# Threshold search moved beside the expert layers: experts run in the order in which they fill, weights by run-time index, token lists by products, the 64-row block in two column groups

## The chip, the cores and the metric

The kernel runs on one core of one Trainium2 chip. Times are device microseconds (us) of one execution. PE is TensorE, PEld its weight load, DVE is VectorE, ACT is ScalarE, POOL is GpSimd.

## The reference

An attention block makes 4608 token vectors of 512 numbers. They are then dealt out to eight experts, each with room for exactly 576 tokens, in the order of all 36,864 scores. Each expert is two matrix products with a ReLU between them. Everything is float32.

```python
def _attn_ref(q, k, v, g_norm):            # q, k, v: (8, 8, 576, 64)
    kv = np.einsum('bhsd,bhse->bhde', k, v)
    out = np.einsum('bhsd,bhde->bhse', q, kv)
    rms = np.sqrt(np.mean(out * out, axis=-1, keepdims=True) + 1e-06)
    return (out / rms * g_norm).astype(np.float32)

def _moe_ref(x, w_gate, w1, w2):           # x: (4608, 512), 8 experts, w1 512x1024, w2 1024x512
    cap = N // E                           # 576
    logits = x @ w_gate
    order = np.argsort(-logits.flatten())
    for idx in order:
        tok, e = (int(idx) // E, int(idx) % E)
        if assigned[tok] >= 0 or counts[e] >= cap:
            continue
        assigned[tok] = e
        counts[e] += 1
    for e in range(E):
        mask = assigned == e
        h = np.maximum(x[mask] @ w1[e], 0.0)
        out[mask] = h @ w2[e]
```

## The kernel before

The kernel never sorts. It does the dealing in eight rounds. In a round each token looks at its best expert that still has room (`choose`). A search then finds the score at which the first expert becomes full (`threshold`), and every choice above that score is accepted (`assign`). So one more expert is full at the end of each of the first seven rounds, and the eighth takes what is left. The search narrows an interval [lo, hi] in eight steps of 16 candidates: DVE compares every token with every candidate, PE counts by 36 small bf16 products (one for each column of 128 tokens), and DVE picks the new interval.

```python
NCAND = 16
NSTEP = 8
# [...] attention; the weights of experts 0 and 1 are requested during it
def threshold():
    lo, hi = bottom, top
    for _ in range(NSTEP):
        step = small("step")
        nc.vector.tensor_scalar(step, in0=hi, scalar1=lo, scalar2=(1.0 + 2.0 ** -18) / (NCAND + 1),
                                op0=AL.subtract, op1=AL.mult)
        cand = small("cand", NCAND)
        nc.vector.tensor_scalar(cand, in0=cand_n, scalar1=step, scalar2=lo, op0=AL.mult, op1=AL.add)
        over = asg.tile([P, GC, NCAND], BF, name="over", tag="over", bufs=2)
        nc.vector.tensor_tensor(over, ..., op=AL.is_ge)      # 36 x NCAND comparisons a partition
        n_ps = psr.tile([NCAND, E], FT, name="n_ps", tag="n", bufs=2)
        for c in range(GC):
            nc.tensor.matmul(n_ps, lhsT=over[:, c, :], rhs=best[:, :, c], start=(c == 0), stop=(c == GC - 1))
        # [...] full, n_full, some: which candidates leave an expert full
        nc.tensor.matmul(k_ps, lhsT=ones_b[0:NCAND, :], rhs=some, start=True, stop=True)
        nc.vector.tensor_scalar(up, in0=k_ps, scalar1=1.0, scalar2=step, op0=AL.add, op1=AL.mult)
        nc.vector.tensor_scalar(hi2, in0=up, scalar1=lo, scalar2=hi, op0=AL.add, op1=AL.min)
        nc.vector.tensor_scalar(lo2, in0=k_ps, scalar1=step, scalar2=lo, op0=AL.mult, op1=AL.add)
        lo, hi = lo2, hi2
    return lo, hi

for _ in range(E - 1):
    choose()
    assign(*threshold())
choose()
# [...] the rest; then the lists of all experts at once by 36 place comparisons and products
gather(0)
gather(1)
turn(0)                                   # transposes of the gathered rows
for e in range(E):
    # first layer: 16 groups of four products, 128x128 by 288, into h_ps
    # turn(e + 1), gather(e + 2)
    for n, (a, nr) in enumerate(blocks):  # second layer: blocks of 128, 128, 128, 128, 64 rows
        for f in range(FC):               # FC = 8
            nc.tensor.matmul(y_ps[0:nr, :], lhsT=hid[:, f, a:a + nr], rhs=w2[:, f, :],
                             start=(f == 0), stop=(f == FC - 1))
        # [...] copy, scatter of the rows to the output
    if e + 2 < E:
        load_w(e + 2)
```

## Time and profile before

| | before |
|---|---|
| median of 4 runs, us | 1035.39 (1034.42 to 1037.18) |
| span of the profiled run, us | 1034.2 |
| attention, us | 0 to 174 |
| search and lists, first gather, us | 174 to 481 |
| experts, us | 481.0 to 1024.2, 67.9 each |
| PE busy over the span | 73% |

The profile has a page with one row per engine over 40 equal slices of the span, a view by stretches and a timeline. A timeline line reads: start, duration, engine, source line, operation, output and inputs, sizes, how many instructions were merged. In brackets stands how long the engine had been idle just before, and what ended the wait. Products are named by the tile that they write, `h_ps` in the first layer and `y_ps` in the second, for example. Merged durations run to the end of the last instruction, which overlaps the next group, so I take costs from start to start. A float32 product shows as two instructions.

### The profile page before, as it was taken

The numbers are of one execution on the slowest core, as the hardware profiler recorded it, in microseconds if no ns is written. First come the engines' busy times: TensorE is split into PE (matmuls) and PEld (weight loads), VectorE is DVE, ScalarE is ACT, GpSimd is POOL, SyncE is SP. The second block draws the span as 40 slices with busy tenths as digits, with TensorE's granted clock in tenths as the row PEclk, the third lists the DMA queues.
The fourth block names the chain that finished last, engine by engine and source line by source line (L and its number), as shares of the span: only waits on it lengthen the run. The fifth ranks groups of instructions, "written<-read, shape, count | busy, mean of one in ns | idle before, by whom it ended". The sixth has DMA issues, their size and how long they took to land.

```text
span 1034.2 us, 13718 instructions
## 1 busy us (share of the span) xinstructions
PE 750.4 (73%) x5917; PEld 499.6 (48%) x5917; DVE 341.8 (33%) x1060; ACT 104.1 (10%) x206; POOL 135.2 (13%) x117
## 2 busy tenths in 40 slices
PE   1888882322322322317999999999999999999996
PEld 1777772221221221215746647557466474574752
DVE  0277556567567567582101101101001011010100
ACT  0144432000000000000100101001011001010100
POOL 2144323000000000005020210211102101001001
PEclk9899996555555555556999999999999999999998
DMA  9998982000000000004032312321223112301000
GB/s 221 297 240 278 320 331 110 1 2 1 1 1 1 2 1 1 1 1 137 24 135 97 137 35 83 147 107 67 91 97 138 65 52 103 107 0 41 6 20 25
DMA packets 32572, 91.07 MB, mean 88 GB/s; under 512 B 2816, under 2 KB 2816, under 8 KB 32512
## 3 DMA queue, kind: packets, MB, share of 16 engines
q1 hardware_dynamic: 24832, 66.59, 19.5%
q0 software_dynamic: 6976, 23.60, 7.2%
q8 instruction: 46, 0.75, 0.3%
q10 hardware_dynamic: 704, 0.02, 0.1%
q14 instruction: 14, 0.11, 0.0%
HBM read 71.32 MB, written 18.87 MB: 87 GB/s over the span
## 4 chain that ended last, share of the span: by engine, by line
issue 49%; DVE 23%; PE 15%; POOL 7%; DMA 4%; ACT 1%; POOLq 0%; DVEq 0%; ACTq 0%
PE n_ps L310 6%; DVE over L305 4%; POOL out_dram L510 4%; DMA v_sb<-in_v_dram 3%; PE o_ps L162 3%; PE kv_ps L131 3%; POOL xg L469 2%; DVE cand L303 2%; DVE part L182 2%; DVE up L320 1%; DVE step L300 1%; DVE hi L322 1%; DVE lo L324 1%; PE qt_ps L155 1%; DVE full L313 1%
## 5 line engine op out<-in xcount | busy, mean ns | idle before, releaser
L506 PE MATMUL y_ps<-w_sb,hid 128*128 128x512 f32 (+1 forms) x640 | 280.2, 594 | 0.0
L496 PE MATMUL h_ps<-xt,w_sb 128*128 128x288 f32 x1024 | 252.3, 408 | 0.9 <-DVE hid L458 0.9
L496 PEld LDWEIGHTS h_ps<-xt,w_sb 128*128 128x128 f32 x1024 | 194.6, 191 | 60.1 <-issue 5.7
L506 PEld LDWEIGHTS y_ps<-w_sb,hid 128*128 128x128 f32 (+1 forms) x640 | 112.5, 179 | 151.3 <-issue 150.7
L310 PE MATMUL n_ps<-best,over 128*16 128x8 bf16 x2016 | 62.6, 176 | 146.3 <-DVE over L305 105.7
L310 PEld LDWEIGHTS <-over 128*16 128x16 bf16 x2016 | 56.9, 90 | 174.1 <-DVE over L305 172.4
L458 DVE TENSOR_SCALAR hid<-h_ps 128x288 f32<-128x288 f32 x64 | 29.2, 458 | 255.1 <-PE h_ps L496 255.1
L469 POOL DMA_INDIRECT xg<-x_dram,ids x40 | 38.1, 952 | 452.5 <-DVE ids L435 296.4
L510 POOL DMA_INDIRECT out_dram<-y_sb,ids x40 | 38.6, 966 | 323.1 <-ACT y_sb L456 189.3
L462 DVE COPY y_sb<-y_ps 128x512 f32<-128x512 f32 (+1 forms) x17 | 11.8, 691 | 208.3 <-PE y_ps L506 208.3
L131 PE MATMUL kv_ps<-v_sb,k_sb 64*64 64x64 f32 x1152 | 45.0, 240 | 27.5 <-DMA v_sb<-in_v_dram 25.9
L131 PEld LDWEIGHTS kv_ps<-v_sb,k_sb 64*64 64x64 f32 x1152 | 42.1, 154 | 30.8 <-issue 27.3
L162 PE MATMUL o_ps<-bd,qt 128*64 128x144 f32 x576 | 46.6, 304 | 10.9 <-DVE qt L157 8.9
L452 ACT ACTIVATE hid<-h_ps 128x288 f32<-128x288 f32 x64 | 26.3, 411 | 223.6 <-PE h_ps L496 223.6
L162 PEld LDWEIGHTS o_ps<-bd,qt 128*64 128x64 f32 x576 | 38.4, 144 | 15.0 <-ACT o_sb L166 8.8
L454 ACT ACTIVATE xt<-t_ps,g_col 128x512 f32<-128x512 f32 (+1 forms) x17 | 11.5, 675 | 324.0 <-PE t_ps L480 321.8
L305 DVE TENSOR_TENSOR over<-mx,cand 128x576 bf16<-128x576 f32 x56 | 42.3, 755 | 1.5
L456 ACT COPY y_sb<-y_ps 128x512 f32<-128x512 f32 (+1 forms) x23 | 13.4, 584 | 253.3 <-PE y_ps L506 253.3
L177 POOL TENSOR_TENSOR x_sb<-o_sb,inv 128x1536 f32<-128x1536 f32 x12 | 33.2, 2769 | 41.6 <-DVE inv L175 32.4
L313 DVE SCALAR_TENSOR_TENSOR full<-n_ps,goal 16x8 f32<-16x8 f32 x56 | 8.6, 153 | 67.7 <-PE n_ps L310 67.7
L480 PEld LDWEIGHTS t_ps<-ident,xg 128*128 128x128 f32 (+1 forms) x160 | 18.7, 149 | 17.9 <-issue 8.0
L460 DVE TENSOR_SCALAR xt<-t_ps,g_col 128x512 f32<-128x512 f32 (+1 forms) x23 | 15.4, 669 | 35.8 <-PE t_ps L480 33.8
(136 smaller groups left out, 471.2 us busy)
## 6 DMA issues: line engine op xcount, KB each, us to landing
w_sb<-in_moe_w_dram SPq DMA_DIRECT2D x16, 2048.0 KB, 9.7
k_sb<-in_k_dram SPq DMA_DIRECT2D x8, 1152.0 KB, 9.6
v_sb<-in_v_dram SPq DMA_DIRECT2D x8, 1152.0 KB, 17.8
x_dram<-x_sb SPq DMA_DIRECT2D x12, 768.0 KB, 4.3
q_sb<-in_q_dram POOLq DMA_DIRECT2D x4, 1152.0 KB
q_sb<-in_q_dram SPq DMA_DIRECT2D x4, 1152.0 KB, 17.3
xg<-x_dram,ids POOLq DMA_INDIRECT x40
out_dram<-y_sb,ids POOLq DMA_INDIRECT x40
```

The lines of the kernel that those rows point to most:

```text
L131: nc.tensor.matmul(kv_ps[ls, r, :], lhsT=k_sb[ls, r, j, :], rhs=v_sb[ls, r, j, :], start=(j == 0), stop=(j == R - 1))
L162: nc.tensor.matmul(o_ps[ps_, r, 0:W], lhsT=qt[:, r, ps_], rhs=bd[:, 2 * i + n, r], start=True, stop=True)
L177: nc.gpsimd.tensor_tensor(x_sb.rearrange("p (a l d) -> p a l d", l=2, d=D), o_sb.rearrange("p t r w -> p (t r) w")[:, :, 0:P].rearrange("p ...
L182: nc.vector.tensor_tensor(part, o_sb.rearrange("p t r w -> p (t r) w")[:, :, P:W].rearrange("p a (l e) -> p a l e", l=2), inv.rearrange("p ...
L305: nc.vector.tensor_tensor(over, mx.rearrange("p (c o) -> p c o", o=1).to_broadcast([P, GC, NCAND]), cand.rearrange("p (o n) -> p o n", o=1 ...
L310: nc.tensor.matmul(n_ps, lhsT=over[:, c, :], rhs=best[:, :, c], start=(c == 0), stop=(c == GC - 1))
L452: nc.scalar.activation(dst, src, ACT.Relu)
L458: nc.vector.tensor_scalar(dst, in0=src, scalar1=0.0, scalar2=None, op0=AL.max)
L469: nc.gpsimd.indirect_dma_start(out=xg[0:nr, :], out_offset=None, in_=x_dram, in_offset=bass.IndirectOffsetOnAxis(ap=ids[0:nr, e * NB + n:e ...
L496: nc.tensor.matmul(h_ps, lhsT=w1[:, d, f * P:(f + 1) * P], rhs=xt[:, d, cs], start=(d == 0), stop=(d == DC - 1))
L506: nc.tensor.matmul(y_ps[0:nr, :], lhsT=hid[:, f, a:a + nr], rhs=w2[:, f, :], start=(f == 0), stop=(f == FC - 1))
L510: put = nc.gpsimd.indirect_dma_start(out=out, out_offset=bass.IndirectOffsetOnAxis(ap=ids[0:nr, e * NB + n:e * NB + n + 1], axis=0), in_=y ...
```

## The change

The intent is to hide the search. An expert's tokens are known as soon as its round is over, so its layers can run while DVE looks for the next threshold. The order in which the experts run is then not known when the program is built, hence weights by an index that is read at run time. Five parts belong to it:

- The search takes 6 steps of 44 candidates in place of 8 of 16, and each step picks lo and hi from precomputed distances (`away`) by two selections, in place of five dependent small operations.
- Each expert gets its own token list, by a running count, a mask and five products (`fetch`).
- Control code is written as Python generators. The layers hand out an estimate of PE time after each product; when the estimated time of a `yield` is used up, the next piece of the search is put into PE's order. That order is then fixed.
- The transposes for the next expert (`turn`) stand together before the last block, and their eviction is on ACT alone.
- The last block of an expert has 64 rows; it is called the half block below. Its eight products are split into two sums of four, in two halves of the array's columns, and DVE adds the halves.

```diff
-NCAND = 16
-NSTEP = 8
+NCAND = 44
+NSTEP = 6
# [...] load_w and the weights' early loads in the attention go away
-        for _ in range(NSTEP):
-            step = small("step")
-            nc.vector.tensor_scalar(step, in0=hi, scalar1=lo, ...)
-            cand = small("cand", NCAND)
-            nc.vector.tensor_scalar(cand, in0=cand_n, scalar1=step, scalar2=lo, op0=AL.mult, op1=AL.add)
+        for s in range(NSTEP):
+            cand = small("cand", NCAND + 2)
+            nc.vector.tensor_scalar(cand[:, 0:NCAND + 1], in0=away[:, s], scalar1=lo, scalar2=None, op0=AL.add)
# [...]
+            nc.vector.tensor_copy(cand[:, NCAND + 1:NCAND + 2], hi)
+            yield 6.5 if s == 0 else 2.9
# [...] 36 products into n_ps; full, some
+            yield 0.9
# [...] k_ps; then up, hi2, lo2 go away for
+            nc.vector.scalar_tensor_tensor(at, in0=row_f[:, 0:NCAND + 1], scalar=k_ps, in1=cand[:, 0:NCAND + 1],
+                                           op0=AL.is_equal, op1=AL.mult, accum_out=lo)
# [...] and the same for hi
+    def fetch(t):
# [...] which expert has filled, its tokens, their running count kn
+        e = nc.sync.value_load(index[0:1, 0:1], min_val=0, max_val=E - 1)
+        w1 = wpool.tile([P, DC, F], FT, name="w1_sb", tag="w1")
+        for h in range(2):
+            fs = slice(h * F // 2, (h + 1) * F // 2)
+            nc.sync.dma_start(w1[:, :, fs], moe_w1[bass.ds(e, 1)]...)
+        w2 = wpool.tile([P, FC, DM], FT, name="w2_sb", tag="w2")
+        nc.sync.dma_start(w2, moe_w2[bass.ds(e, 1)].rearrange("o (a p) d -> p (o a) d", p=P))
+        yield 3.0
+        nc.tensor.matmul(a_ps, lhsT=before, rhs=kn[:, GC - 1:GC], start=True, stop=True)
# [...]
+        yield 2.4
+        for n in range(NB):
+            nc.tensor.matmul(s_ps[:, n], lhsT=of[:, n * P:(n + 1) * P], rhs=kn, start=True, stop=True)
# [...] ids from s_ps; five indirect gathers
+            if n == NB - 1 and t + 1 < E:
+                yield None                    # the turn of the next expert comes here
# [...] whole blocks as before; the block of 64 rows:
+                for f in range(FC // 2):
+                    for l in range(2):
+                        nc.tensor.matmul(y_ps[l * nr:(l + 1) * nr], lhsT=hid[:, l * FC // 2 + f, a:a + nr],
+                                         rhs=w2[:, l * FC // 2 + f, :], start=(f == 0), stop=(f == FC // 2 - 1))
+                nc.scalar.copy(y_part, y_ps[nr:2 * nr])
+                nc.vector.tensor_tensor(y_sb[0:nr], y_ps[0:nr], y_part, op=AL.add)
# [...]
+    for _ in control(0):
+        pass
+    for _ in turn(0):
+        pass
+    with tc.manual_schedule(engines={PE, DVE, Activation}):    # (names shortened)
+        for t in range(E):
+            ctl = control(t + 1) if t + 1 < E else None
+            wait = next(ctl, None) if ctl is not None else None
+            for used in layers(t):
+                if used is None:
+                    while wait is not None:
+                        wait = next(ctl, None)
+                    for _ in turn(t + 1):
+                        pass
+                    continue
+                if wait is not None:
+                    wait -= used
+                    if wait <= 0:
+                        wait = next(ctl, None)
```

## The prediction

> **What bounds the kernel now.** I read the page's slice rows first: they show three stages that barely overlap. In this fence each digit is one fortieth of the span (25.9 us).
>
> ```profile
> PE   1888882322322322317999999999999999999996
> DVE  0277556567567567582101101101001011010100
> PEclk9899996555555555556999999999999999999998
> DMA  9998982000000000004032312321223112301000
> ```
>
> Attention fills slices 0 to 6. Then come twelve slices in which PE is 20 to 30% busy at half the clock, DVE is 50 to 80% busy and DMA is at zero: the search for the eight experts' thresholds. Then PE is full to the end. The stretch view puts numbers on it (columns: stretch, length, busy time and count of PE, weight loads, DVE, ACT, POOL, then granted clock, DMA share, GB/s):
>
> ```profile
> 174.00:180.50 6.50, 0.66 (x2) 0.29 (x2) 6.07 (x35) 0.00 (x0) 0.16 (x1) 0.50 0.00 0
> 180.50:470.00 289.50, 79.78 (x2123) 67.18 (x2123) 195.71 (x756) 0.00 (x0) 0.00 (x0) 0.50 0.00 1
> 470.00:481.00 11.00, 6.01 (x23) 4.02 (x23) 1.50 (x2) 1.40 (x3) 7.97 (x9) 0.50 0.54 152
> 481.00:1024.20 543.20, 542.34 (x1802) 321.30 (x1802) 54.19 (x101) 49.84 (x102) 67.85 (x71) 1.00 0.22 78
> ```
>
> So 296 us go to setup, search and lists, 11 us to the first gather, 543 us to experts in which PE never waits (542.3 of 543.2), and 10 us to the last write. Search and experts stand in line only because the program orders them so: the first is a chain of small dependent steps, the second is bound by PE. One step of the search, from the timeline (start, duration, engine, line):
>
> ```profile
> 203.06 0.76 DVE L305 TENSOR_TENSOR over<-mx,cand 128x576 bf16<-128x576 f32 x1
> 203.87 1.12 PE L310 MATMUL n_ps<-best,over 128*16 128x8 bf16 x36 [2.05 <-DVE over L305]
> ...
> 205.03 0.15 DVE L313 SCALAR_TENSOR_TENSOR full<-n_ps,goal 16x8 f32<-16x8 f32 x1 [1.21 <-PE n_ps L310]
> ...
> 205.42 0.16 PE L318 MATMUL k_ps<-some,ones_b 16*128 16x1 bf16 x1 [0.43 <-DVE some L316]
> ```
>
> The comparison of the step before starts at 199.30, so a step takes 3.76 us. The last view is one expert on PE, again the timeline; matmuls of f32 are two instructions each:
>
> ```profile
> 549.50 0.14 PEld L506 LDWEIGHTS y_ps<-w_sb,hid 128*64 128x64 f32 x1 [0.29 <-issue]
> 550.45 31.31 PE L496 MATMUL h_ps<-xt,w_sb 128*128 128x288 f32 x128
> 585.55 33.03 PE L506 MATMUL y_ps<-w_sb,hid 128*128 128x512 f32 x76
> 618.50 1.72 PE L496 MATMUL h_ps<-xt,w_sb 128*128 128x288 f32 x6
> ```
>
> 550.45 to 618.50 is 68.05 us: 64 first-layer products at 0.487 (31.1), 40 second-layer products at 0.858 (34.3), 20 transposes in about 2.1, and gaps. The fifth block has 64 rows, yet its eight products start 0.43 us per instruction apart, just as full blocks do: 6.9 us for half the work.
>
> **What the Trainium skill says.** "TensorE: Matmul & The Clock Gate", Part 1, says that an idle PE is clocked at half and that about 3.4 us of sustained work releases it. The trace agrees: 0.50 in the search, 1.00 in the experts. Search products placed inside the expert stream should therefore run at full clock, while the first search stays at half. The same page, Part 2 (LDWEIGHTS), has the load cost grow with the columns of the stationary operand; the search's operand grows from 16 to 44 columns. At half clock the trace has 36 pairs in 1.12 us, 31 ns a pair, for 16 columns; no 44-column load is in it. Part 3 says that products of at most 64 output rows in different column groups run at once. The trace supports it: the attention's `o_ps` products (64 columns, 144 wide) alternate halves and 16 instructions take 1.20 us, 75 ns each, whereas 144 wide at the experts' 0.429 us per 512 would alone be 121 ns. "TensorEngine Tiling (Array Packing)", Key Properties, warns that a change of tiling mode drains PE; no row before isolates that, and I allow for it below.
>
> **The change part by part.**
>
> *First search, still exposed.* 44 candidates and six steps replace 16 and eight. The comparison grows from 576 to 1584 elements; the rows with 576 (755 ns) and 1440 elements (1651 ns) give 1.04 ns an element, so 1.80 us. The counting burst at half clock I put at 1.6 us (44-column load plus 8 columns, about 43 ns a pair). Counting and its follow-up (full, some, `k_ps`, two selections with accumulators, new candidates, a copy) are 1.6 us. A step is 5.05 us, six are 30.3. Setup grows from 6.5 to 8 us (a POOL iota and six `away` rows). The assignment takes 3.3 us to its product; then, because the scheduler weaves the next choose into it on DVE, 6.3 us to `a_ps`, 3.2 to `s_ps`, and 4.3 to the list, of which one 1.8 us comparison is woven in. That is 8 + 30 + 17 = 55 us from 174 us: list at 229. Gather and transposes then take 11 us as before: experts start at 240 instead of 481. Weights, which used to be fetched in the attention, are asked for some 10 us before the list is done; 4 MB land in about 20 us (9.7 us per 2 MB), about when they are needed. Lists for all experts at once (the 36 place comparisons and products, 457 to 470 us) go away.
>
> *Seven searches inside the experts.* They no longer add their chain, only their PE time and any wait at which PE's in-order stream meets an unfinished DVE step. PE time: six bursts at 1.25 us (36 pairs at some 30 ns, plus a drain at each end), six `k_ps` at 0.1, and the rest 0.5: 8.6 us. Waits: by the order of the built program, 14 first-layer products (6.8 us) stand before the first burst, against about 7.2 us of DVE (merge of the half block, choose, comparison); six products (2.9 us) against 2.9 between steps; five second-layer ones before `all_ps`, enough; four (3.4 us) before `a_ps`, against some 5.5 us of DVE. I take 3.0 us of waits.
>
> *Half block in two.* Sixteen instructions in pairs: about 3.8 us instead of 6.9.
>
> *Transposes together, evictions on ACT alone.* Five blocks through two banks at 0.69 us each on ACT, behind a 0.58 us output copy: 3.5 us instead of 2.1. ACT has about 13 us of work per expert, so it does not bound.
>
> Per expert: 31.0 + 27.5 (32 full products) + 3.8 + 3.5 + 8.6 + 3.0 = 77.4 us. Expert 0 pays about 2 us for the rising clock, as before; six with a search come to 466. Expert 6 carries only the remainder's list, whose `a_ps` stands after seven products (3.4 us) while DVE needs some 8.5: 72 us. Expert 7 carries nothing: 62.3. Together 600 us, against 543.
>
> *Tail.* 10.0 us before, plus 0.8 for the copy and addition of the two halves.
>
> Sum: 240 + 600 + 11 = 851 us; I say **850**. The search gives 241 us back, its presence among the experts costs about 82, the half block returns about 25 of that.
>
> **The rivals.** First, PE is the bound of the expert stage, so whatever is put there adds. If a burst drains PE at both ends or a 44-column load is not hidden, it costs 2 us instead of 1.25: 42 bursts add 32 us, 882. For: no such mix is in the trace, and mode changes drain. Against: the bursts run at full clock. Second, PE's order is now fixed; if DVE is late by 0.5 us at each of some 60 meeting points, that adds 30 us, and a gap beyond 3.4 us could halve the clock for a window. For: the budgets are close to my DVE sums. Against: each product of spacing only has to absorb what I counted. Third, weights by run-time index may land late, because they are asked for only some 48 us into the expert before (41 to `all_ps` and 7 of DVE and queue). 4 MB in 20 us end near 70, needed at 77: hidden, unless scatter and gather double it; then about 10 us per expert, 920. Fourth, the other way: the half block pairs well, bursts cost 1.0 us and waits vanish, and it is 820. A loss of the whole gain would need the experts to take 100 us each; nothing points to it.
>
> **Range and chances.** The first search is good to 8 us, the bursts to 15, waits to 12, the half block to 8; together about 25 either way, and the upper side has more ways. Range 825 to 885. Faster by over 2% means under 1014, which is 160 us away: 0.97. Within 2% 0.015, slower 0.015.
>
> **What would show it.** In the changed kernel's timeline: a step of the first search of 5 us and the first continuous `h_ps` near 240; granted clock 1.0 afterwards; expert to expert 77 us; a burst of 36 about 1.25 us between two `h_ps`; half block under 4 us; the waits on PE naming DVE mainly at `a_ps` and the first burst; no PE wait for `w_sb`. I am wrong if `h_ps` waits for weights, if a burst takes 2 us or more, if the half block still takes 6.9, or if the first search takes well over 55 us.

## The result, and the profile after

The changed kernel takes **847.8 us** (median of 4 runs, 847.21 to 848.48), the kernel before 1035.39. The ratio is 0.819 (95% interval 0.817 to 0.820). A ratio here is the mean time of one kernel's runs over the mean of the other's in the same rounds, so it is not quite the quotient of the medians.

The slice rows of the changed kernel's page (a slice is 21.2 us here):

```profile
PE   0689889513099999999999999999999997999995
DVE  0064854855725505633570555156235605000000
PEclk9899999855599999999999999999999998999998
DMA  9999892100610430070016005300800264200000
```

The stretch of sparse PE at half clock has shrunk from twelve slices to three. From the twelfth slice on PE is full at full clock, and DVE is busy beside it. The 7 in PE's row, near the end, is one slice in which something went wrong; it returns below. DMA is at 6 of 10 in the eleventh slice, where the kernel before had none: the first weights and the first rows.

The stretches (length, then busy time and count of PE, PEld, DVE, ACT, POOL, then clock, DMA share, GB/s):

```profile
174.00:184.22 10.22, 0.66 (x3) 0.29 (x3) 9.30 (x42) 0.00 (x0) 1.45 (x3) 0.50 0.00 0
184.22:210.28 26.06, 10.57 (x222) 9.73 (x223) 14.26 (x53) 0.00 (x0) 0.00 (x0) 0.50 0.00 1
210.28:231.00 20.72, 0.70 (x8) 0.39 (x8) 16.27 (x60) 0.00 (x0) 2.78 (x3) 0.50 0.54 197
231.00:237.30 6.30, 4.05 (x21) 3.34 (x21) 0.00 (x0) 2.55 (x4) 2.08 (x3) 0.59 0.60 207
237.30:835.70 598.40, 579.43 (x3191) 351.67 (x3190) 208.72 (x711) 96.01 (x204) 71.00 (x74) 0.99 0.22 79
```

The experts begin at 237.3 in place of 481.0: 243.7 us gained. They take 598.4 us in place of 543.2: 55.2 us given back. The tail is 10.3 in place of 10.0. That is the whole difference of the spans, 1034.2 to 846.0.

PE's timeline shows where the 55.2 us are. First two bursts of the exposed search, then a piece of the first expert with its bursts, then the end of that expert:

```profile
184.22 1.60 PE L323 MATMUL n_ps<-best,over 128*44 128x8 bf16 x36 [6.61 <-DVE over L316]
...
188.99 1.60 PE L323 MATMUL n_ps<-best,over 128*44 128x8 bf16 x36 [2.57 <-DVE over L316]
...
245.30 1.24 PE L506 MATMUL h_ps<-xt,w_sb 128*128 128x288 f32 x4
246.47 0.17 PE L332 MATMUL k_ps<-some,ones_b 44*128 44x1 bf16 x1
246.57 3.18 PE L506 MATMUL h_ps<-xt,w_sb 128*128 128x288 f32 x12
249.68 1.13 PE L323 MATMUL n_ps<-best,over 128*44 128x8 bf16 x36
250.74 1.24 PE L506 MATMUL h_ps<-xt,w_sb 128*128 128x288 f32 x4
...
284.05 0.16 PE L423 MATMUL a_ps<-know,before 128*128 128x1 bf16 x1 [1.70 <-DVE index L412]
...
307.55 1.04 PE L485 MATMUL t_ps<-ident,xg 128*128 128x128 f32 x8
...
310.80 3.65 PE L525 MATMUL y_ps<-w_sb,hid 128*64 128x512 f32 x16
```

An exposed step is 188.99 − 184.22 = 4.77 us. Among the layers the burst takes 250.74 − 249.68 = 1.06 us and the `k_ps` product 0.10. But the four `h_ps` instructions after a burst take 246.47 − 245.30 = 1.17 us, where four at the usual 0.243 would take 0.97, and the twelve after `k_ps` take 3.11, where twelve would take 2.92. So each excursion from the float32 stream to small products and back costs 0.2 us beside the products themselves, and a step costs PE 1.06 + 0.10 + 2 × 0.2 = 1.56 us.

Narrow windows of the same timeline show single instructions, and where the 0.2 us lie:

```profile
246.13 0.41 PE L506 MATMUL h_ps<-xt,w_sb 128*128 128x288 f32 x1
246.47 0.17 PE L332 MATMUL k_ps<-some,ones_b 44*128 44x1 bf16 x1
...
246.92 0.41 PE L506 MATMUL h_ps<-xt,w_sb 128*128 128x288 f32 x1
...
277.76 1.02 PE L517 MATMUL y_ps<-w_sb,hid 128*128 128x512 f32 x2
278.62 0.17 PE L363 MATMUL all_ps<-sums,ones_b 128*128 128x16 bf16 x1
```

About half is lost on the way in: `k_ps` starts 246.47 − 246.13 = 0.34 us after the last `h_ps`, where another `h_ps` starts after 0.243. The other half is lost on the way back: the first `h_ps` starts at 246.57, and the second 0.35 us later. The type is not what costs on the way in. `all_ps`, also bf16 but 128 by 128 like the stream, starts 0.43 us after the last `y_ps`, the usual distance; the `y_ps` after it costs 0.08. And the 28 `h_ps` that follow a float32 half block (314.39 to the next burst at 321.38) also take 0.2 us more than their 6.80, with no bf16 product before them. The loss on the way in thus goes with a change of the stationary operand's shape (44 columns, 44 rows or 64 columns in place of 128 by 128).

The turn takes 310.80 − 307.55 = 3.25 us. The half block takes 3.6 us; the next expert begins at 314.39. PE waits 1.70 us for DVE before `a_ps` in each of the first six experts, and no longer anywhere else in them than 0.4 us at the turn. The half blocks of experts 0 and 5 begin at 310.80 and 696.43, so one expert takes 385.63 / 5 = 77.13 us.

Expert 6, which prepares the last list without a search, has a gap:

```profile
700.02 3.66 PE L506 MATMUL h_ps<-xt,w_sb 128*128 128x288 f32 x14
708.32 0.16 PE L423 MATMUL a_ps<-know,before 128*128 128x1 bf16 x1 [4.64 <-DVE index L412]
708.34 5.15 PE L506 MATMUL h_ps<-xt,w_sb 128*128 128x288 f32 x10
713.28 0.37 PE L437 MATMUL s_ps<-know,of 128*128 128x39 bf16 x5
```

PE stands still for 4.64 us, and the next ten `h_ps` instructions take 5.15 us where ten take 2.67 without the gap (shown with an experiment below). The clock was halved: the view by stretches has 0.50 from 707.3 to 713.9 us, and 1.00 before and after. The gap costs about 7 us in all.

The sum of an ordinary expert, from these lines: 64 first-layer products 31.1, 32 whole second-layer products 27.5, half block 3.6, turn 3.25, six steps 9.4, other small products about 0.6, wait at `a_ps` 1.7. That is 77.1, against 67.9 before. Six such experts are 462.8, expert 6 takes 73.3, expert 7, beside which nothing runs, 62.3.

### The profile page after: what moved, and what is told of

Its sections match the earlier page's. It is cut to its first block, busy times and chain, and to the rows that moved or that the text cites. A ratio compares the mean times of both kernels' runs of the same rounds, so it can differ in the third digit from the quotient of the medians.

```text
span 846.0 us, 12815 instructions
## 1 busy us (share of the span) xinstructions
PE 714.9 (85%) x5410; PEld 470.7 (56%) x5410; DVE 332.4 (39%) x1033; ACT 152.1 (18%) x310; POOL 136.5 (16%) x119
## 4 chain that ended last, share of the span: by engine, by line
PE 59%; issue 16%; DVE 13%; DMA 6%; ACT 3%; POOL 2%; ACTq 0%; SPq 0%; POOLq 0%; DVEq 0%
PE h_ps L506 24%; PE y_ps L517 17%; PE n_ps L323 6%; DMA v_sb<-in_v_dram 4%; PE o_ps L162 3%; PE y_ps L525 3%; PE kv_ps L131 2%; DVE part L182 2%; DMA w_sb<-in_moe_w_dram 1%; DVE over L316 1%; DVE ms L167 1%; ACT xt L486 1%; PE qt_ps L155 1%; POOL out_dram L490 1%; PE t_ps L485 1%
## 5 line engine op out<-in xcount | busy, mean ns | idle before, releaser
L506 PE MATMUL h_ps<-xt,w_sb 128*128 128x288 f32 x1024 | 273.0, 417 | 0.0
L517 PE MATMUL y_ps<-w_sb,hid 128*128 128x512 f32 x512 | 224.6, 595 | 0.0
L517 PEld LDWEIGHTS y_ps<-w_sb,hid 128*128 128x128 f32 x512 | 95.8, 190 | 124.0 <-issue 123.2
L509 ACT ACTIVATE hid<-h_ps 128x288 f32<-128x288 f32 x128 | 52.5, 410 | 260.1 <-PE h_ps L506 258.5
L316 DVE TENSOR_TENSOR over<-mx,cand 128x1584 bf16<-128x1584 f32 x42 | 75.9, 1808 | 1.3
L323 PE MATMUL n_ps<-best,over 128*44 128x8 bf16 x1512 | 50.2, 178 | 19.5 <-DVE over L316 19.5
L323 PEld LDWEIGHTS <-over 128*44 128x44 bf16 x1512 | 46.1, 104 | 36.6 <-DVE over L316 22.7
L131 PE MATMUL kv_ps<-v_sb,k_sb 64*64 64x64 f32 x1152 | 43.0, 235 | 27.5 <-DMA v_sb<-in_v_dram 27.5
L520 ACT COPY y_sb<-y_ps 128x512 f32<-128x512 f32 x32 | 18.7, 585 | 216.3 <-PE y_ps L517 216.3
L485 PE MATMUL t_ps<-ident,xg 128*128 128x128 f32 (+1 forms) x160 | 23.2, 283 | 14.2 <-DMA xg<-x_dram,ids 9.8
L525 PE MATMUL y_ps<-w_sb,hid 128*64 128x512 f32 x128 | 29.2, 598 | 0.0
## 6 DMA issues: line engine op xcount, KB each, us to landing
w_sb<-in_moe_w_dram SPq DMA_DIRECT2D x8, 2048.0 KB, 17.3
```

The source lines that it names most:

```text
L131: nc.tensor.matmul(kv_ps[ls, r, :], lhsT=k_sb[ls, r, j, :], rhs=v_sb[ls, r, j, :], start=(j == 0), stop=(j == R - 1))
L316: nc.vector.tensor_tensor(over, mx.rearrange("p (c o) -> p c o", o=1).to_broadcast([P, GC, NCAND]), cand[:, 1:NCAND + 1].rearrange("p (o n ...
L485: nc.tensor.transpose(t_ps[:, d, 0:nr], xg[0:nr, d * P:(d + 1) * P], ident[0:nr, 0:nr])
L506: nc.tensor.matmul(h_ps, lhsT=w1[:, d, f * P:(f + 1) * P], rhs=xt[:, d, cs], start=(d == 0), stop=(d == DC - 1))
L509: nc.scalar.activation(hid[:, f, cs], h_ps, ACT.Relu)
L517: nc.tensor.matmul(y_ps, lhsT=hid[:, f, a:a + nr], rhs=w2[:, f, :], start=(f == 0), stop=(f == FC - 1))
```

## The experiments

Theory: the gain is the overlap alone. The search that is left beside the experts costs PE about 1.5 us a step, and the half block earns some of that back. Rivals: the gain comes from a cheaper search (44 candidates, six steps, new arithmetic), which would have helped the old order too; or it comes from the half block. Twelve kernels ran, on three chips, each set with runs of the kernel before on the same chip. The changed kernel itself ran only with its first set, so a difference from it below goes across chips; medians of the kernel before in the four sets lie within 1.1 us of each other (1034.3 to 1035.4). All twelve results agree with the reference, the one with the coarse search included.

### serial: the overlap alone undone

```diff
-            wait = next(ctl, None) if ctl is not None else None
+            if ctl is not None:
+                for _ in ctl:
+                    pass
+            wait = None
```

Everything else of the change stays, but each search runs to its end before the layers of the expert.

> The changed kernel with one thing undone: each search runs to its end before the layers of the expert before it start, so nothing of it lies beside the experts' products; every other part stays. Theory (the overlap is the gain): a search alone is about 48 us of chain (choose 4, six steps of 4.77, assignment and list some 15), against 11.7 us that it costs now among an expert's products (77.1 less 65.4 of pure work); six searches give +218, the remainder's list +8, and restarting at half clock +2 to 3 each, so about 1090 us. Rival (the gain comes from fewer steps, cheaper lists and the split half block, the overlap being eaten by contention on PE): 870 to 930 us.

Measured: 1050.93 us, ratio to before 1.015 (1.013 to 1.017). The timeline between expert 0 and expert 1 (the half block of the one, the first burst, the list, the layers of the next):

```profile
332.88 3.65 PE L525 MATMUL y_ps<-w_sb,hid 128*64 128x512 f32 x16
343.22 1.60 PE L323 MATMUL n_ps<-best,over 128*44 128x8 bf16 x36 [6.69 <-DVE cand L319]
...
378.24 0.16 PE L423 MATMUL a_ps<-know,before 128*128 128x1 bf16 x1 [5.47 <-DVE index L412]
```

The layers go on at 380.68, so the chain takes 44.2 us from the end of the half block at 336.5. I had expected 48. From it come off the 10 us of PE time and the 1.7 us of waits that an expert no longer has among its products, which leaves 32.5 us. The layers then start at half clock (0.50 from 380.7 to 385.2 us), as I had also counted on: the 128 first-layer products take 32.6 us in expert 0 and up to 34.1 later, where 31.1 is usual. So an expert with a search takes 111.1 to 112.5 us in place of 77.1, 34.0 to 35.4 more. Five of these (174.6) and a first expert that begins 32.3 us later are 207 us. The last list, for which I had expected 8 us more, gives 3.3 back, because expert 6 then has neither a gap nor a list among its products. The spans differ by 203.6. Of the 39 us that I had expected too much, about 26 lie in the six searches and 11 in the last list. What follows: the overlap is worth 203 us, more than the whole gain of 187. Without it, the rest of the change is slower than the kernel before.

### before_44x6 and before_newstep: the search alone, in the old order

The first puts 44 candidates and six steps into the kernel before, and nothing else. The second adds the new arithmetic (`away`, two selections).

```diff
-NCAND = 16
-NSTEP = 8
+NCAND = 44
+NSTEP = 6
```

> The kernel before with 44 candidates and six steps in place of 16 and eight, nothing else. Theory: a step grows from 3.76 to about 4.8 us, 42 in place of 56 steps, so 201 against 210 us of search: about 1026 us, 1% faster. Rival (fewer steps are what saved the time): 56 to 42 steps at an unchanged 3.76 would give 982 us.

Measured: 1048.1 us, ratio 1.012 (1.010 to 1.014). This is a miss in sign. The timeline of this kernel, two bursts:

```profile
188.10 1.60 PE L310 MATMUL n_ps<-best,over 128*44 128x8 bf16 x36 [3.11 <-DVE over L305]
...
193.42 1.60 PE L310 MATMUL n_ps<-best,over 128*44 128x8 bf16 x36 [3.12 <-DVE over L305]
```

A step is 5.31 us, not the 4.77 of the changed kernel: the old chain of small operations (`up`, `lo`, `hi`, `step`, `cand`) is still in it. 42 steps of 5.31 are 223 us, 56 of 3.76 were 211. A wider step costs more than the two steps it saves. The next kernel tests this reading.

> The kernel before with the whole step of the changed kernel: 44 candidates, six steps, and the two selections in place of five small dependent operations. Theory: a step is 4.77 us instead of the 5.31 of the run with 44 by six alone, so 42 steps are 200 us against 210 before, less a microsecond for setup: about 1026 us. Rival (the extra 13 us of that run came from elsewhere): about 1048.

Measured: 1028.14 us, ratio 0.995 (0.993 to 0.998), and a step of 4.77 us. So the new arithmetic takes 0.54 us out of a step, 23 us in 42 steps (20 us are measured against before_44x6, on another chip), and the two together bring the old order 6 us. The cheaper search explains next to nothing of the 187.

### sixteen_by_eight: the changed kernel with the old numbers

```diff
-NCAND = 44
-NSTEP = 6
+NCAND = 16
+NSTEP = 8
```

> The changed kernel with 16 candidates and eight steps, as before the change. Theory (a burst of 36 pairs costs PE nearly the same for 16 columns as for 44, so two more steps add 1.56 us each in six searches, 19 us; the first search is eight steps of about 3.2, 3 us shorter): about 864 us. Rival (the load's columns decide; a 16-column burst costs a good deal less than 1.06 us): 850 or below.

Measured: 866.92 us, ratio 0.838 (0.837 to 0.840), 19 us more than the changed kernel. Its burst among the layers:

```profile
327.81 1.12 PE L323 MATMUL n_ps<-best,over 128*16 128x8 bf16 x36
328.85 1.24 PE L506 MATMUL h_ps<-xt,w_sb 128*128 128x288 f32 x4
```

328.85 − 327.81 = 1.04 us for 16 columns, and 1.06 us for 44. At full clock the width of the candidates costs PE nothing, and the change to small products and back costs the same 0.2 us. An expert takes 80.8 us, 3.7 more: two steps at 1.56, and about 0.6 because the turn now waits for its rows. So 44 by 6 is worth its wider comparison only where the comparison is hidden. In the exposed first search of this kernel a step takes 3.16 us, so eight steps take 25.3 us where six of 4.77 take 28.6, and the first expert begins 4.1 us sooner, at 233.14. With the old arithmetic 44 by 6 lost in the old order too.

### three_steps: half the search

```diff
-    def threshold():
+    def threshold(steps):
# [...] and control(t) calls threshold(NSTEP if t == 0 else 3)
```

> The changed kernel with only three steps in the seven later searches (the first but all six of the first search remain); thresholds are too coarse, so the result is wrong on purpose, the lists stay valid. 18 steps go (six later searches of six steps hold steps: 36 to 18). Theory (each step adds its PE time to a stream that PE bounds, 1.56 us by the timeline: 1.06 burst, 0.11 second product, 0.2 at each of two re-entries into f32): 28 us less, about 820 us. With my predicted 1.35 us a step: 24 us less, 824. Rival (the bursts fill gaps of PE or DVE sets the pace): under 8 us less.

Measured: 817.98 us, ratio 0.790 (0.788 to 0.791), 29.8 us less. Divided by the 18 steps that went, this is 1.66 us each, but not all of it is theirs. From expert to expert it is 72.47 us in place of 77.13, which is 1.55 us a step: the 1.56 to which the timeline's terms add up, and not the 1.35 that I had predicted. The rest lies in the start (0.4 us) and in expert 6 (1.1 us), which has the same gap of 4.64 us but spends 3.4 us at half clock after it, where the changed kernel spends 6.8. On these inputs the result stayed within tolerance, but a threshold this coarse lets the order of tokens decide inside the last interval, so this is no usable version.

### half_whole: the split of the 64-row block undone

```diff
-            if nr == P:
+            if True:
-                    nc.tensor.matmul(y_ps, lhsT=hid[:, f, a:a + nr], rhs=w2[:, f, :],
+                    nc.tensor.matmul(y_ps[0:nr], lhsT=hid[:, f, a:a + nr], rhs=w2[:, f, :],
-                nc.scalar.copy(y_sb, y_ps)
+                nc.scalar.copy(y_sb[0:nr], y_ps[0:nr])
```

> The changed kernel with the 64-row block as eight whole products, as before. Theory: the split saves 6.9 less 3.6 us for each of eight experts, less 0.6 us of tail, so about 873 us. Rival (the second copy and the addition, or a drain at the mode change, give it back): within 5 us of 848.

Measured: 867.71 us, ratio 0.838 (0.837 to 0.840), 19.9 us more. The block in the timeline:

```profile
310.24 7.08 PE L517 MATMUL y_ps<-w_sb,hid 128*64 128x512 f32 x16
```

7.0 us in place of 3.6, 3.4 an expert, as expected, and 8 × 3.4 would be 27. The rest has another cause: here expert 6 has no gap at `a_ps` and takes 69.3 us, 4 less than in the changed kernel although its half block is longer. The split puts an addition of the halves into DVE's fixed order just ahead of the next list, so DVE can't begin that list before the half block is done; without the split it can. The split is a gain of 20 us net, and a tenth of the change's gain, not its source.

### later_ahead: PE meets the list later

The gap at `a_ps` suggests a budget that is too small: the layers hand out 3.0 us of products, DVE needs more.

```diff
-        yield 3.0
+        yield 5.2 if t < E - 1 else 8.5
```

> The changed kernel with its one schedule number changed that stands before the product a_ps: 5.2 us of PE work (8.5 for the remainder's list) instead of 3.0, so that DVE is done when PE comes to it. Theory: the wait of 1.70 us in each of six experts goes (10 us), and the 4.6 us gap in the seventh expert with the slow products after it (together 7.5 us by its length, 73.3 us, against 69.25 where the gap was absent and the block was 3.4 us longer) goes too: about 830 us. Rival (the wait only moves, to s_ps, to the gather or to the transposes): within 5 us of 848.

Measured: 829.21 us, ratio 0.802 (0.800 to 0.803), 18.6 us less. In expert 6:

```profile
698.34 0.17 PE L423 MATMUL a_ps<-know,before 128*128 128x1 bf16 x1
698.37 2.67 PE L506 MATMUL h_ps<-xt,w_sb 128*128 128x288 f32 x10
```

No wait stands before `a_ps`, in any expert, and the ten instructions after it run at full clock in 2.67 us. Six waits of 1.7 are 10.2 us and the gap with its slow clock about 7; that is 17 of the 18.6. The change of a number in the schedule gives a tenth of the whole gain again.

### turn_between: the transposes among products

```diff
-            if n == NB - 1 and t + 1 < E:
+            if n == NB - 2 and t + 1 < E:
# [...] in the main loop, where the turn was run to its end:
-                    for _ in turn(t + 1):
-                        pass
+                    turning = turn(t + 1)
+                if turning is not None:
+                    next(turning, None)           # one block after each product
```

> The changed kernel with the transposes for the next expert laid one block at a time between the products of the fourth block, instead of all at once before the half block. Theory: ACT's 0.69 us a block is then hidden behind 0.86 us products and 20 transposes cost their 2.1 us instead of 3.25: 1.1 us for each of seven experts, about 840 us. Rival (each return from transposes to products costs, or the gathered rows are not there yet): 848 or above.

Measured: 841.06 us, ratio 0.813 (0.812 to 0.814), 6.7 us less:

```profile
301.34 0.60 PE L485 MATMUL t_ps<-ident,xg 128*128 128x128 f32 x4
301.78 1.02 PE L517 MATMUL y_ps<-w_sb,hid 128*128 128x512 f32 x2
```

Four transposes cost 0.44 us now, with no wait for ACT between blocks. An expert takes 76.31 us in place of 77.13. So a turn gains 0.82 us net, less than the 1.1 us that I had expected, since the last block has 64 rows and pays for two changes of shape among the products. Seven turns are 5.7 of the 6.7 us. Expert 6 gains another 1.1, because its stretch at half clock is 3.4 us long and not 6.8.

### first_in_order and all_three: the first search in the fixed order

```diff
-    for _ in control(0):
-        pass
-    for _ in turn(0):
-        pass
     with tc.manual_schedule(...):
+        for _ in control(0):
+            pass
+        for _ in turn(0):
+            pass
```

The scheduler had woven the next `choose` into the end of the first search. This keeps it out. The kernel all_three has this edit with the two edits above.

> The changed kernel with the first search and the first transposes also held in program order on PE, DVE and ACT, so that the next search's choose and comparison no longer stand in front of the first list. Theory: the list is ready about 3.5 us earlier (0.5 before a_ps, 0.6 before s_ps, 1.8 for the comparison, 0.12 a step for the copy), about 844 us. Rival (program order exposes read-after-write gaps that the scheduler had filled): 848 or above.

> The three edits together. Theory: they take time from different places and add up, 17 + 8 + 3.5: about 820 us. Rival (with the earlier transposes, the later a_ps leaves the gather no slack and PE waits for rows): 825 to 840.

Measured: first_in_order 850.72 us, ratio 0.823 (0.821 to 0.824), 3 us **more** than the changed kernel; all_three 826.64 us, ratio 0.799 (0.798 to 0.801). Both are misses. The list is indeed ready 2.7 us sooner, at 224.63 in place of 227.33, but the rows as a whole do not land sooner: the first transposes start at 231.76 in place of 232.96, those of the last block at 237.61 in place of 236.87. In first_in_order (stretches, with DMA share and GB/s at the end):

```profile
225.00:230.00 5.00, 0.00 (x0) 0.00 (x0) 4.72 (x13) 0.00 (x0) 3.97 (x4) 0.50 1.04 381
230.00:235.00 5.00, 2.83 (x11) 2.06 (x12) 1.13 (x2) 1.38 (x2) 1.66 (x1) 0.50 1.04 397
```

DMA is full there. The weights of the first expert, 4 MB, are asked for at 220.65 in this kernel, 2 us later than in the changed one (218.73), and the 1.1 MB of rows share the engines with them. Besides, the transposes come in pieces as the rows land, the clock stays at half, and the first 28 `h_ps` instructions take 9.95 us in place of 7.06. The reading is thus that transfers, not the list, set the start of the first expert; four_edits tests it below.

### two_edits and four_edits

The kernel two_edits has later_ahead and turn_between alone. The kernel four_edits has all three edits, and tests the reading above: the second-layer weights of the first expert are taken out of the way of the rows.

```diff
-        nc.sync.dma_start(w2, moe_w2[bass.ds(e, 1)]...)
+        if t > 0:
+            nc.sync.dma_start(w2, moe_w2[bass.ds(e, 1)]...)
# [...] and after turn(0), on ACT's queue:
+        e0 = nc.scalar.value_load(weights["index"][0:1, 0:1], min_val=0, max_val=E - 1)
+        nc.scalar.dma_start(weights[0][1], moe_w2[bass.ds(e0, 1)]...)
```

> The later a_ps and the transposes between products, without the first search in program order. Theory: 829.2 less the 6.7 that the transposes gave alone: about 822.5 us, which would show that program order in the first search is what cost the three edits 4 us. Rival (the two share slack of the gather): 826 or above.

> The three edits, with the first expert's second-layer weights (2 MB) asked for on ACT's queue behind the first transposes instead of on SP's ahead of the gather. Theory (the first experts' start is bound by the DMA engines: 4 MB of weights and 1.1 MB of rows at 380 to 397 GB/s from the moment of the request, so an earlier list gains nothing and the rows come late): with 2 MB out of the way the rows land as fast as they are asked for, the first products start near 234.5 instead of 237 to 238, about 820 us or less, and 6 less than the three edits. Rival (the half clock after the long idle decides): 825 or above with first products where they were.

Measured: two_edits 823.87 us, ratio 0.797 (0.795 to 0.798); one of its runs, the profiled one, took 830.45, with the first expert beginning at 243.49, and the other four 823.2 to 824.7. In that run's trace the first burst of the search already stands at 190.18 in place of the 184.22 of the changed kernel, so its delay arose in the attention, which no edit touches; why is open. The median is 2.8 us under all_three, which fits the loss of 3 us that first_in_order showed. four_edits took 821.88 us, ratio 0.795 (0.794 to 0.797). In its timeline the transposes and the first expert:

```profile
229.58 3.19 PE L488 MATMUL t_ps<-ident,xg 128*128 128x128 f32 x12 [7.07 <-DMA xg<-x_dram,ids]
...
234.81 7.06 PE L509 MATMUL h_ps<-xt,w_sb 128*128 128x288 f32 x28
```

The list comes later than in all_three (225.1 against 223.3), yet the first expert begins at 234.81 in place of 237.10 and its first instructions take 7.06 in place of 9.14 us. That is 4.4 us, and the kernel gained 4.8 over all_three. I had expected 6. The cause holds: 2 MB fewer in flight make the rows land sooner, which is 2.3 us of the 4.4. The other 2.1 are the clock, so the rival is half right: between 235 and 240 us it is 1.00 here and 0.50 in all_three, where the transposes came in pieces. Over two_edits the gain is only 2 us, and it lies close to the spread of the runs.

## Why the prediction was right

The prediction of 850 us, with a range of 825 to 885, stands against 847.8. Its sum holds in all the large terms. Two smaller ones inside an expert, the search on PE and the waits, were off in opposite directions, and so were two around it, the rising clock and expert 6.

- **Bound.** "Search and experts stand in line only because the program orders them so": confirmed by serial, where the same parts in line take 1050.93 us.
- **Start of the experts.** Predicted 240, measured 237.3. The step was put at 5.05 us and is 4.77; the whole first search with its list took 53.3 us (174 to 227.33), predicted 55. The burst at half clock is 1.60 us as predicted, the comparison 1.81. The step is shorter because the follow-up of the count, put at 1.6 us, takes less: 4.77 − 1.81 − 1.60 leaves 1.4 us.
- **Experts' stage.** Predicted 600, measured 598.4; one expert 77.4 against 77.13. The 2 us for a rising clock in expert 0 did not come: its first 28 `h_ps` take 7.06 us, as in expert 1.
- **The search on PE, too small by one term.** The burst was put at 1.25 us, "plus a drain at each end" included; it is 1.06, and 1.26 with the loss at its two ends. That term was right. The `k_ps` product was put at 0.1 us without such a loss, and costs 0.3. A step is thus 1.56 us where 1.35 was written, and three_steps, at 1.55 from expert to expert, says so too. With the other products it is 10 us an expert in place of 8.6. The 31 ns a pair, from which the burst was worked out, is the length of a burst over 36, with the last product's own time in it; the starts lie 27 ns apart.
- **The waits, mis-sized the other way.** 3.0 us an expert were predicted, 1.7 measured. The first burst was expected to wait and did not; `a_ps` was expected to wait and did, in every expert. The two errors, about 1.4 us up and 1.3 down, cancel. The total is right partly by that luck.
- **Expert 6.** Predicted 72 us, with the right cause (seven products stand before `a_ps`, DVE needs 8.5 us); measured 73.3. The second rival had warned that a gap beyond 3.4 us could halve the clock, but no cost for it was in the sum. The trace shows the gap of 4.64 us and ten instructions of 5.15 in place of 2.67; later_ahead shows both gone.
- **Half block and turn.** Predicted 3.8 and 3.5 us, measured 3.6 and 3.25. half_whole shows 7.0 us unsplit. Its net worth of 20 us is under the predicted 25, because the addition on DVE lengthens the gap in expert 6.
- **Weights.** No wait of PE for `w_sb` appears among the experts, as predicted: 1 MB lands in 6.3 us and 2 MB in 17.3, asked for at 285 and needed at 314. The third rival did not come about. But the prediction treated the first expert's weights as hidden too, "about when they are needed". It overlooked that the rows of the first gather share the DMA engines with them, which first_in_order ran into and four_edits shows.

The rivals fall as follows. The first (a burst of 2 us) is refuted by 1.06 us, or 1.26 with both ends. Its sum counts 42 bursts, but only 36 stand beside the experts, since the first search is exposed: it should have read 27 us and 877. (For the same reason the heading "Seven searches inside the experts" should say six, as the sum does.) The second (30 us of waits on top of those counted) did not come about, except for the halved clock in expert 6. All waits at `a_ps` over seven experts are 14.8 us, less than the 18 that the sum held for six alone, as the view of waits has it (who waited for whom, us in total, times, longest):

```profile
PE a_ps L423 <- DVE index L412: 14.8, 7, 4.6
```

The fourth (820 us) was not reached by the change, but two_edits (823.87) and four_edits (821.88) come near it by removing the waits that it named, and in part by moving the transposes. What stays open is what makes the first float32 product after a small one cost 0.1 us more, and why the attention took 6 us longer in one run of two_edits.

## What to carry to other kernels

A chain of small dependent steps costs little when it stands inside a stream that another engine bounds, and this holds even if the steps are made wider for it; price it by what it takes from the bounding engine, the loss on the way in and back included, and not by the chain's length. With a fixed order, give each meeting point a budget from measured durations of the other engine, with some to spare: one such number here was worth a tenth of the gain. When a prefetch moves to a later point, look at what else uses the transfers there, since an earlier request elsewhere may gain nothing.

## What the Trainium skill lacked or had wrong

- "TensorE: Matmul & The Clock Gate", Part 2 (LDWEIGHTS), gives a load time of columns / 1.2 ns, so 37 ns for 44 columns and 13 for 16, and names no clock for it. At full clock the products of a burst start 27 ns apart for both widths, each with its own load between, so 37 ns is too long there. At half clock they start 40 and 27 ns apart.
- The same page, Part 3, has a table of measured speedups for tiles of 32 columns or rows. For two groups of 64 columns, 512 wide, float32, the runs show 3.6 us against 7.0, a factor of 1.95.
- "TensorEngine Tiling (Array Packing)", Key Properties, says that a change of mode drains the engine, without a size. Here a product whose stationary operand has another shape than those before it (44 or 16 columns, 44 rows) starts 0.09 us late, and one that is bf16 but 128 by 128 does not. The float32 product after it costs another 0.10 us, whether 36 small products stand before or one; after a small product of 128 by 128 it costs 0.08. So the loss on the way in fits the drain; what the second one is, no run separates.
- No page gives a size for what a gather of rows loses beside weight loads that were asked for earlier. 1.1 MB of rows beside 4 MB of weights made DMA full at 381 to 397 GB/s, and taking 2 MB away brought the first expert's start from 237.10 (all_three) to 234.81 (four_edits).
